# Attention with local and pooled keys, then a two-layer MLP in fp32r pairs: new constants for the order planner, and the first chunk's scores taken from the loaded k rows

## The chip, the cores and the metric

The kernel runs on one core of a Trainium2 chip. The metric is device time in microseconds (us) of one execution; "time before" is the median of three runs. The profile is one further execution of the same program, with its own time.

## The reference

`q`, `k` and `v` have the shape (4 batches, 8 heads, 768 positions, 64). Each row attends to the keys less than 16 positions away and to 24 pooled keys, one for each block of 32 positions. The MLP then runs on the 3072 rows of 512 numbers.

```python
k_sum = k.reshape(B, H, nb, block, D).max(axis=3)      # 24 pooled keys
v_sum = v.reshape(B, H, nb, block, D).mean(axis=3)     # 24 pooled values
scores_l = scale * q @ k.T                             # kept where |i - j| < 16
scores_s = scale * q @ k_sum.T + log(block)
a = softmax(concat([scores_l, scores_s]))
attn = a @ concat([v, v_sum])
h = attn_rows @ w_in                                   # 3072 x 512 @ 512 x 2048
out = max(0.01 * h, h) @ w_out                         # 3072 x 2048 @ 2048 x 512
```

## The kernel before

**Tiling.** The rows are cut into eight chunks `c` of 384 rows, two for each batch. A chunk has four pairs of heads `p` and three tiles of 128 rows, so 12 units `u` of (pair, tile). For a unit, TensorE makes the scores (`scores`, L371): two heads by two half tiles of 64 rows, each 64 by 120, of which 24 columns are pooled keys and 96 are a window of k. VectorE adds the mask and takes the row minimum (`lowest`, L376), ScalarE exponentiates (`expo`, L383), VectorE divides by the sum (L420, L424, L428), TensorE transposes (`turn`, L388), ScalarE copies the result out (`pt`, L439), TensorE multiplies with the values (`values`, L394), and the product is split into a high and a low fp32r part (`xhi` L445 on ScalarE, `xlo` L448 on VectorE).

**Where the 120 keys come from.** `operands` loads q into the tile `k`, and k into a slot of `big` (named `("kn", c, p)`; six slots of 1024 columns, which also take the raw weights and the raw v). `k_max` (L248, VectorE) reduces the k rows to `ksum`. Then two ScalarE copies (`windows`, L315) lay the overlapping windows of k into the tile `k`, and a VectorE copy (`k_s`, L331) puts the pooled keys in front of each window, so that one matmul of 120 columns reads a contiguous run.

**The values.** For the first batch, TensorE averages v (`v_mean_pe`, L284): three loads `("vb", 0, j)` of 512 KB, two matmuls of 512 columns for each, all into one bank, then a ScalarE copy to `vs` (L289). GpSimd spreads the 24 pooled values into the tile `v` of each pair (`load_s`, L327). `values` cannot run for a pair before that copy. The tiles `e` and `pt` have two buffers for pairs of units, so units cannot run far ahead of `values`.

**The MLP.** `mlp` makes `h` (`m1`, L724), gates it, and accumulates the second product (`m2`, L743 to L745), in the parts of `PARTS`. The weights arrive as raw fp32 (`weights`, one load of 512 KB each, `("w", f, 0)` for w_in and `("w", f, 1)` for w_out) and are split into fp32r pairs by three VectorE operations (L680, L687, L693) and two ScalarE operations (L684, L690). From the third batch position on, products of sums are used (`strassen`), which is the larger part of the time.

**What sets the order.** All instructions are put into a list by `Plan`: each has an engine, a cost in ns and a priority. `Plan.order` runs a list schedule once while the program is built: at each step the engine that is free first takes the ready instruction with the lowest priority number. The time that an instruction gets there fixes its place on its engine; on the chip each engine runs its instructions in that order. Loads are all issued from SyncE (SP) in their order. `Plan.LAT` is the latency that the planner adds from one engine's end to a waiting instruction; a load ends 1200 ns after its issue at the earliest, plus its bytes at `rate`, after the loads before it:

```python
if o["size"]:
    dma = max(dma, end + 1200) + o["size"] / o["rate"]
    end = dma
```

The priorities are made of the unit's place (`PLACE`: for each chunk a start and a step), of offsets for each step of chunks 0 and 1 (`OFF`), and of the constants `PL` to `WO`; `LOADS` fixes the order of the first 20 loads outright. In the gaps that the planner expects on TensorE before the first MLP product, `build` puts small matmuls on zeros (L1343, tile `spare`).

Of the kernel before, what the change touches and what calls it, by code (L numbers as in the profile page):

```python
# [23 lines left out]
LK = 120  # L24
# [41 lines left out]
WT = 1.15
W0 = -1.523
WO = 1.029
CUT = 1
WIDE = 12  # L70
OFF = {('rec', 0): (-2.762, -0.036), ('ex', 0): (3.066, -0.083), ('pt', 0): (0.079, -0.747), ('tr', 0): (-2.274, -0.362), ('ttr', 0): (-5.883, 0.424), ('nrm', 0): (0.274, -0.908), ('qk', 0): (-7.35, 0.368), ('xlo', 0): (1.352, 0.149), ('xhi', 0): (-1.785, 0.164), ('av', 0): (-2.699, -0.545), ('pt', 1): (3.776, 0.667), ('xlo', 1): (2.15, -1.485), ('tr', 1): (-0.4, -0.633), ('ttr', 1): (5.204, 0.013), ('qk', 1): (5.855, -0.039), ('av', 1): (-6.304, -0.442), ('ex', 1): (1.869, -0.057), ('nrm', 1): (1.368, -0.059), ('rec', 1): (3.066, -0.235), ('xhi', 1): (-5.461, -0.101)}
LOADS = [('kn', 0, 0), ('q', 0, 1), ('q', 0, 0), ('kn', 0, 1), ('mask',), ('vb', 0, 0), ('kn', 0, 2), ('vb', 0, 2), ('q', 0, 2), ('vb', 0, 1), ('kn', 0, 3), ('w', 0, 0), ('v', 0, 0), ('v', 0, 1), ('q', 0, 3), ('v', 0, 2), ('v', 0, 3), ('w', 1, 0), ('w', 0, 1), ('w', 1, 1)]


class Plan:


    LAT = {"SP": 910.0, "PE": 200.0, "DVE": 130.0, "ACT": 142.0, "POOL": 190.0,
# [5 lines left out]
    def op(self, eng, cost, prio, fn, after=(), use=(), alloc=(), size=0, rate=250.0, port=False):  # L84
# [26 lines left out]
    def order(self):  # L111
# [18 lines left out]
        while any(cand.values()):  # L130
# [14 lines left out]
            if o["size"]:  # L145
                dma = max(dma, end + 1200) + o["size"] / o["rate"]
                end = dma
# [16 lines left out]
def DVE(n, fast=False):  # L164
    return 65 + (0.52 if fast else 1.042) * n
# [6 lines left out]
def build(tc, ctx, a):  # L172
# [126 lines left out]
    def operands(c, p, t, ahead):  # L299
# [36 lines left out]
        ks = [P.op("ACT", ACT(TPC * 96), t - 0.6 + (0 if b else XW), lambda j=j: windows(j), after=[lq, kn_op[kw]], use=[kk, kw]) for j in range(2)]  # L336
# [5 lines left out]
        ks.append(P.op("DVE", DVE(2 * TPC * NS, True), t - 0.5 + (0 if b else KS), k_s, after=[lq, ksum_op[b, p]], use=[kk, ("ksum", b, p)]))  # L342
# [58 lines left out]
    def unit(u):  # L401
# [48 lines left out]
        o = P.op("PE", 480, v + 0.1 + off("qk"), qk, after=k_op[c, p], use=[kk], alloc=[("h", K("s0"), 0), ("h", K("s1"), 0)] if wide else [("s0", K("s0"), 1), ("s1", K("s1"), 1)])  # L450
        z = []
        for h in range(2):
            al = [(x, (x, m), ER) for x in "emz"] if h + u % 2 == 0 else []
            z.append(P.op("DVE", 280, v + 0.2 + off("ttr"), lambda h=h: lowest(u, h, tl[K(f"s{h}")][:, :LK]), after=[o, mask_op] + z[:1] + first_of.get(m, []),
# [3 lines left out]
        rc = P.op("DVE", 120, v + 0.45 + off("rec"), guard, after=e, use=[("z", m)])  # L458
        rc = P.op("DVE", 130, v + 0.5 + off("rec"), rec, after=[rc], use=[("z", m)])
# [937 lines left out]
```

## Time and profile before

| | us |
|---|---|
| median of three runs | 613.66 |
| lowest and highest | 612.68, 614.12 |
| the profiled execution, its own time | 612.7 |
| its span, first to last instruction | 610.9 |

The 1.8 us between the profiled execution's time and its span lie outside the instructions. The profile lists busy time by engine: PE is TensorE's matmuls, PEld its weight loads, DVE VectorE, ACT ScalarE, POOL GpSimd, SP SyncE, whose entries are issues of DMAs. The ends of matmuls are modelled, so their durations overlap: the time that one costs is read from the start of one to the start of the next. An fp32 matmul leaves two entries. Matmuls on zeros count as busy, so PE's busy share alone does not tell how much of its time is work.

### The profile page before, as it was taken

The page shows a single profiled execution, that of the slowest core. Times are in us where ns is not written, and L with a number is a line of the kernel's source. Part 1 is how long each engine was busy: PE and PEld are TensorE (multiplying, and loading weights), DVE is VectorE, ACT ScalarE, POOL GpSimd, SP SyncE. Part 2 cuts the span into 40 slices and gives each one's busy share as a digit, 9 for nine tenths or more (in the row PEclk, how much of TensorE's full clock was granted, in tenths as well). Part 3 has the DMA queues.
Part 4 walks back from the last instruction along what each step waited for, and adds up shares of the span by engine and source line. Part 5 has one row for each costly group of instructions (what it writes and reads, how often), then busy time and mean ns, then how long its engine had stood idle before and what let it go on. Part 6 is the DMA issues. An engine that isn't in the chain of part 4 may idle for free.

```text
span 610.9 us, 12895 instructions
## 1 busy us (share of the span) xinstructions
PE 604.9 (99%) x4676; PEld 540.1 (88%) x4676; DVE 469.7 (77%) x1281; ACT 351.1 (57%) x965; POOL 4.4 (1%) x10
## 2 busy tenths in 40 slices
PE   9999999999999999999999999999999999999997
PEld 6688889889888889999898897989889899999996
DVE  5899999953989995536688875877987783868687
ACT  5899996553776676416466665753717262606060
POOL 0200000000000000000000000000000000000000
PEclk9999999999999999999999999999999999999999
DMA  8898998896878826526497563866757484757552
GB/s 298 245 282 273 288 301 245 269 325 198 288 240 244 252 64 197 167 65 190 120 292 229 175 219 120 280 202 216 257 183 231 143 236 143 237 152 229 156 155 103
DMA packets 82926, 129.99 MB, mean 213 GB/s; under 512 B 7024, under 2 KB 50608, under 8 KB 82864
## 3 DMA queue, kind: packets, MB, share of 16 engines
q1 hardware_dynamic: 82864, 129.18, 68.1%
q8 instruction: 37, 0.61, 0.4%
q14 instruction: 25, 0.20, 0.1%
HBM read 97.72 MB, written 29.36 MB: 208 GB/s over the span
## 4 chain that ended last, share of the span: by engine, by line
PE 91%; DVE 4%; ACT 2%; DMA 1%; issue 0%; SPq 0%; DVEq 0%
PE L L1229 19%; PE h L724 12%; PE X L1090 8%; PE W L1090 8%; PE Z L1090 7%; PE B_a L1040 5%; PE a L744 4%; PE a L745 4%; PE a L743 4%; PE Y L1090 4%; PE B_s L1040 2%; PE B_to L1040 1%; ACT e L383 1%; PE vps L284 1%; DMA big<-in_k_dram 1%; DVE big L687 1%
## 5 line engine op out<-in xcount | busy, mean ns | idle before, releaser
L724 PE MATMUL h<-x,win_hi 128*128 128x384 f32 x320 | 82.7, 339 | 0.0
L383 ACT ACTIVATE e<-e,m 128x120 f32<-128x120 f32 x192 | 73.7, 388 | 3.7 <-DVE m L376 3.5
L1229 PE MATMUL L<-wout_hi,win_hi 128*128 128x512 f32 x168 | 66.5, 396 | 0.0
L1229 PE MATMUL L<-wout_hi,win_lo 128*128 128x512 f32 x168 | 65.7, 391 | 0.0
L1229 PE MATMUL L<-wout_lo,win_hi 128*128 128x512 f32 x168 | 65.6, 391 | 0.0
L724 PEld LDWEIGHTS h<-x,win_hi 128*128 128x128 f32 x320 | 57.6, 188 | 2.3 <-issue 0.2
L724 PE MATMUL h<-x,win_lo 128*128 128x384 f32 x160 | 53.8, 336 | 0.0
L743 PE MATMUL a<-wout_hi,ghi 128*128 128x512 f32 x120 | 48.4, 403 | 0.0
L745 PE MATMUL a<-wout_hi,glo 128*128 128x512 f32 x120 | 47.3, 394 | 0.0
L744 PE MATMUL a<-wout_lo,ghi 128*128 128x512 f32 x120 | 47.1, 392 | 0.1
L1229 PEld LDWEIGHTS L<-wout_hi,win_lo 128*128 128x128 f32 x168 | 31.5, 188 | 6.8
L383 ACT ACTIVATION_READ_ACCUMULATOR e<-e,m 128x1 f32 x192 | 36.7, 191 | 0.0
L1229 PEld LDWEIGHTS L<-wout_lo,win_hi 128*128 128x128 f32 x168 | 31.6, 188 | 5.7
L1229 PEld LDWEIGHTS L<-wout_hi,win_hi 128*128 128x128 f32 x168 | 31.6, 188 | 5.7
L734 DVE TENSOR_TENSOR glo<-gs,ghi 128x384 fp32r<-128x384 f32 x40 | 22.1, 554 | 17.0 <-ACT gs L728 16.3
L731 ACT ACTIVATE ghi<-h 128x384 fp32r<-128x384 f32 x40 | 19.6, 490 | 25.9 <-PE h L724 25.9
L1186 ACT COPY P<-X 128x384 f32<-128x384 f32 x19 | 9.0, 473 | 37.0 <-PE X L1090 36.9
L724 PEld LDWEIGHTS h<-x,win_lo 128*128 128x128 f32 x160 | 30.0, 188 | 0.0
L745 PEld LDWEIGHTS a<-wout_hi,glo 128*128 128x128 f32 x120 | 22.5, 188 | 5.4 <-DVE glo L734 0.4
L315 ACT COPY k<-big 128x288 f32<-128x288 f32 x64 | 24.8, 434 | 4.1 <-DMA big<-in_k_dram 4.0
L744 PEld LDWEIGHTS a<-wout_lo,ghi 128*128 128x128 f32 x120 | 22.6, 188 | 3.9 <-DVE wout_lo L693 0.4
L743 PEld LDWEIGHTS a<-wout_hi,ghi 128*128 128x128 f32 x120 | 22.6, 188 | 3.3
(620 smaller groups left out, 1625.9 us busy)
## 6 DMA issues: line engine op xcount, KB each, us to landing
win_hi<-sums SPq DMA_DIRECT2D x73, 256.0 KB
win_lo<-sums SPq DMA_DIRECT2D x71, 256.0 KB
big<-in_w_dram SPq DMA_DIRECT2D x32, 512.0 KB
sums<-big SPq DMA_DIRECT2D x32, 512.0 KB
v<-in_v_dram SPq DMA_DIRECT2D x32, 288.0 KB
big<-in_k_dram SPq DMA_DIRECT2D x16, 400.0 KB
k<-in_q_dram SPq DMA_DIRECT2D x32, 192.0 KB
wout_hi<-sums SPq DMA_DIRECT2D x21, 256.0 KB
```

Source lines behind the costliest of these rows:

```text
L315: nc.scalar.copy(k, x)
L383: nc.scalar.activation(out=e[:, n], in_=e[:, n], func=AF.Exp, scale=-1.0, bias=m[:, n:n + 1], accum_out=z[:, n:n + 1])
L724: nc.tensor.matmul(h[:, :T], w[:, 512 * f + 128 * k:512 * f + 128 * k + 128], x[:, T * k:T * k + T], start=n == 0, stop=n == 11)
L731: nc.scalar.activation(out=gnew(tag, G("ghi", f)), in_=tl[G("h", f)][:, :T], func=AF.Prelu, alpha=0.01)
L734: nc.vector.tensor_tensor(out=gnew(tag, G("glo", f)), in0=tl[G("gs", f)], in1=tl[G("ghi", f)].bitcast(F32), op=ALU.subtract)
L743: nc.tensor.matmul(o, gh, wout_hi[:, f], start=f == f0, stop=False)
L744: nc.tensor.matmul(o, gh, wout_lo[:, f], start=False, stop=False)
L745: nc.tensor.matmul(o, gl, wout_hi[:, f], start=False, stop=f == f1 - 1)
L1040: nc.tensor.matmul(o[:, x:x + 256], g, w[l], start=fresh and m == 0, stop=m == 5, skip_group_check=True)
L1090: nc.tensor.matmul(o[:, :T], w[:, l, 128 * k:128 * k + 128], x[y][:, T * k:T * k + T], start=start and n == 0, stop=n == 5, skip_group_che ...
L1186: nc.scalar.copy(tmp(K("P1")), ps("X"))
L1229: nc.tensor.matmul(o, g, w[:, f], start=s + m == 0, stop=s == 1 and m == 5)
```

## The change

Three things are done at once.

- The planner's numbers: the end of a load is counted from 1900 ns after its issue instead of 1200, with 60 ns of latency behind it instead of 910, and bytes at 297 per ns instead of 250 (290 for weights). The VectorE costs of `lowest` (280 to 215), of the guard (120 to 90) and of the reciprocal (130 to 90) go down.
- In chunk 0 (`c == 0`), `windows` and `k_s` are left out. `scores` makes each block of 64 by 120 with two matmuls: 96 columns straight from the loaded k rows in `big`, and 24 columns from `ksum`. The scores wait for the two loads and for `k_max`; the slot of `big` and the tile `ksum` are held until they have run. Their planned cost is 640 ns instead of 480.
- `PLACE`, `OFF`, `LOADS` and the constants `CV`, `PG`, `P2` and `PL` to `WO` have new values; `LOADS` begins with other loads. The new numbers and costs hold for the whole program, so that every engine's order can differ.

```diff
-PLACE = {0: (0.0, 1.0), 1: (13.07, 0.61), 2: (24.128751, 0.979249), 3: (33.570341, 0.464868), ...
+PLACE = {0: (-0.56363, 1.023761), 1: (13.941805, 0.493885), 2: (24.006994, 0.724777), 3: (33.542294, 0.443354), ...
...
-VT = -1.915
-KP = -1.757
+VT = -2.297378
+KP = -2.510813
...
-OFF = {('rec', 0): (-2.762, -0.036), ... ('tr', 0): (-2.274, -0.362), ... ('qk', 0): (-7.35, 0.368), ... ('av', 0): (-2.699, -0.545), ...
+OFF = {('rec', 0): (-9.400226, -0.966702), ... ('tr', 0): (2.239967, -0.883064), ... ('qk', 0): (-4.669325, 0.548837), ... ('av', 0): (-0.911237, -0.250157), ...
-LOADS = [('kn', 0, 0), ('q', 0, 1), ('q', 0, 0), ('kn', 0, 1), ('mask',), ('vb', 0, 0), ('kn', 0, 2), ('vb', 0, 2), ('q', 0, 2), ('vb', 0, 1), ('kn', 0, 3), ('w', 0, 0), ('v', 0, 0), ('v', 0, 1), ('q', 0, 3), ('v', 0, 2), ('v', 0, 3), ('w', 1, 0), ('w', 0, 1), ('w', 1, 1)]
+LOADS = [('kn', 0, 2), ('q', 0, 0), ('mask',), ('kn', 0, 0), ('vb', 0, 0), ('kn', 0, 1), ('q', 0, 1), ('vb', 0, 1), ('vb', 0, 2), ('kn', 0, 3), ('q', 0, 2), ('v', 0, 0), ('v', 0, 1), ('w', 0, 0), ('q', 0, 3), ('v', 0, 2), ('v', 0, 3), ('w', 0, 1), ('w', 1, 0), ('w', 1, 1)]
...
-    LAT = {"SP": 910.0, "PE": 200.0, ...
+    LAT = {"SP": 60.0, "PE": 200.0, ...
...
-    def op(self, ..., size=0, rate=250.0, port=False):
+    def op(self, ..., size=0, rate=297.0, port=False):
...
-                dma = max(dma, end + 1200) + o["size"] / o["rate"]
+                dma = max(dma, end + 1900) + o["size"] / o["rate"]
...
-        ks = [P.op("ACT", ACT(TPC * 96), ..., lambda j=j: windows(j), ...) for j in range(2)]
+        ks = [P.op("ACT", ACT(TPC * 96), ..., lambda j=j: windows(j), ...) for j in range(2)] if c else [lq, kn_op[kw], ksum_op[b, p]]
...
-        ks.append(P.op("DVE", DVE(2 * TPC * NS, True), ..., k_s, ...))
+        if c:
+            ks.append(P.op("DVE", DVE(2 * TPC * NS, True), ..., k_s, ...))
...
                 n, w = 128 * i + 64 * j, T + KC * i + LK * j
+                if c == 0:
+                    o = s[h][64 * j:64 * j + 64, col:col + LK]
+                    nc.tensor.matmul(o[:, NS:], k[x, n:n + 64], tl["kn", c, p][x, n:n + LK - NS], start=True, stop=True)
+                    nc.tensor.matmul(o[:, :NS], k[x, n:n + 64], tl["ksum", c, p][x], start=True, stop=True)
+                    continue
                 nc.tensor.matmul(s[h][64 * j:64 * j + 64, col:col + LK], k[x, n:n + 64], k[x, w:w + LK], start=True, stop=True)
...
-        o = P.op("PE", 480, v + 0.1 + off("qk"), qk, after=k_op[c, p], use=[kk], ...)
+        o = P.op("PE", 640, v + 0.1 + off("qk"), qk, after=k_op[c, p], use=[kk, ("kn", c, p), ("ksum", c, p)], ...)
...
-        o = load_op(("w", f, w), ..., size=128 * 4096, rate=290.0)
+        o = load_op(("w", f, w), ..., size=128 * 4096)
```

## Rows read from the trace of the kernel before

**Rows 1.** The page: its head and the busy time of the engines over the whole span.

```profile
span 610.9 us, 12895 instructions
...
PE 604.9 (99%) x4676; PEld 540.1 (88%) x4676; DVE 469.7 (77%) x1281; ACT 351.1 (57%) x965; POOL 4.4 (1%) x10
```

**Rows 2.** Busy time by stretch. Columns: the stretch and its length in us, busy us (and instructions) of PE, PEld, DVE, ACT and POOL, granted TensorE clock, share of the DMA engines' time, GB/s.

```profile
5.00:8.00 3.00, 2.84 (x55) 2.40 (x52) 1.31 (x5) 0.77 (x3) 0.00 (x0) 1.00 1.02 377
8.00:16.00 8.00, 7.85 (x81) 4.09 (x81) 6.04 (x42) 6.67 (x30) 0.00 (x0) 1.00 0.96 330
16.00:21.56 5.56, 5.56 (x46) 2.48 (x46) 4.62 (x20) 3.52 (x13) 0.98 (x2) 1.00 1.03 250
21.56:34.00 12.44, 12.41 (x195) 9.49 (x193) 10.49 (x50) 11.72 (x45) 2.68 (x3) 1.00 0.83 246
34.00:60.00 26.00, 25.92 (x200) 22.19 (x198) 24.92 (x82) 24.80 (x72) 0.00 (x0) 1.00 0.92 281
60.00:100.00 40.00, 40.00 (x283) 35.14 (x282) 39.49 (x94) 35.64 (x82) 0.00 (x0) 1.00 0.93 284
...
233.00:500.00 267.00, 267.00 (x1907) 238.46 (x1906) 191.50 (x483) 142.81 (x383) 0.00 (x0) 1.00 0.63 196
```

**Rows 3.** The same view for the matmuls on zeros alone (L1343). Columns: stretch, length, busy us of PE and of PEld, clock, DMA share, GB/s.

```profile
5.00:21.56 16.56, 5.61 (x87) 4.92 (x84) 1.00 0.99 312
21.56:34.00 12.44, 2.44 (x35) 1.93 (x33) 1.00 0.83 246
```

**Rows 4.** The timeline of PE around the first `values` and the last matmuls on zeros. Columns: start us, length us, engine, line, operation, tiles, shapes, count.

```profile
19.84 1.79 PE L1343 MATMUL spare<-zero 128*128 128x128 bf16 x29
21.56 0.69 PE L394 MATMUL o<-pt,v 120*64 120x64 f32 x16
...
33.21 0.95 PE L1343 MATMUL spare<-zero 128*128 128x128 bf16 x14
33.97 0.63 PE L724 MATMUL h<-x,win_hi 128*128 128x384 f32 x2
```

**Rows 5.** The timeline of the first 24 us: the way from the pooled values' matmuls to the tile `v`. A bracket gives the idle time of the engine before the row and what ended it.

```profile
15.34 1.04 PE L284 MATMUL vps<-big,mask 128*24 128x512 f32 x2
...
18.01 1.90 PE L284 MATMUL vps<-big,mask 128*24 128x512 f32 x4
...
19.94 0.57 ACT L289 COPY vs<-vps 24x512 f32<-24x512 f32 x1 [1.51 <-PE vps L284]
...
20.58 3.66 POOL L327 COPY v<-vs 24x768 f32<-24x768 f32 x4 [19.28 <-ACT vs L289]
```

**Rows 6.** Waits of TensorE's weight loads over the whole span: who waited for whom, us in total, times, longest us.

```profile
PEld B_a L1040 <- DVE y L1051: 0.7, 1, 0.7
```

**Rows 7.** The timeline of the DMA issues on SP.

```profile
4.02 0.56 SPq L278 DMA_DIRECT2D big<-in_v_dram  x1
8.87 0.33 SPq L310 DMA_DIRECT2D k<-in_q_dram  x1
9.24 0.43 SPq L278 DMA_DIRECT2D big<-in_v_dram  x1
...
11.29 0.90 SPq L319 DMA_DIRECT2D v<-in_v_dram  x2
```

**Rows 8.** Bytes of the loads, from the list of DMA issues: count, KB each.

```profile
v<-in_v_dram SPq DMA_DIRECT2D x32, 288.0 KB
big<-in_k_dram SPq DMA_DIRECT2D x16, 400.0 KB
k<-in_q_dram SPq DMA_DIRECT2D x32, 192.0 KB
...
big<-in_v_dram SPq DMA_DIRECT2D x3, 512.0 KB
...
mask<-in_mask_dram SPq DMA_DIRECT2D x1, 202.0 KB
```

**Rows 9.** The first 15 us in the view by stretch, with the columns of Rows 2.

```profile
0.00:5.00 5.00, 4.01 (x48) 4.02 (x49) 1.18 (x3) 2.05 (x3) 0.70 (x6) 1.00 0.65 199
5.00:10.00 5.00, 4.82 (x73) 3.29 (x70) 3.13 (x21) 2.77 (x13) 0.00 (x0) 1.00 1.00 380
10.00:15.00 5.00, 4.87 (x55) 2.90 (x58) 3.64 (x21) 3.67 (x15) 0.00 (x0) 1.00 0.93 311
```

**Rows 10.** The timeline of the start: the first two maxima of k, the first scores and the first mask.

```profile
3.90 0.95 DVE L248 TENSOR_REDUCE ksum<-big 128x24 f32<-128x768 f32 x1 [2.97 <-DMA big<-in_k_dram]
...
5.86 0.64 PE L371 MATMUL s<-k 64*64 64x120 f32 x16
...
6.81 0.95 DVE L248 TENSOR_REDUCE ksum<-big 128x24 f32<-128x768 f32 x1 [1.69 <-DMA big<-in_k_dram]
7.68 0.27 DVE L376 CUSTOM_DVE_ANT_0 e<-s,mask 128x120 f32<-128x120 f32 x1
```

**Rows 11.** ScalarE's groups of instructions between 21.56 and 34 us: the copies that lay out the windows. Columns behind the first bar: busy us, mean ns of one; behind the second: idle time before them.

```profile
L315 ACT COPY k<-big 128x288 f32<-128x288 f32 x4 | 1.6, 437 | 0.0
```

**Rows 12.** VectorE's groups in the same stretch: the copies that lay out the pooled keys.

```profile
L331 DVE COPY k<-ksum 128x144 f32<-128x144 f32 x2 | 0.5, 228 | 0.0
```

**Rows 13.** Two neighbours on PE's timeline: one unit's scores, and what starts behind them.

```profile
23.83 0.44 PE L371 MATMUL s<-k 64*64 64x120 f32 x8
24.20 0.45 PE L394 MATMUL o<-pt,v 120*64 120x64 f32 x8
```

More of the change, by code (lines that the diff above doesn't have):

```diff
@@ L82, in __init__, with op @@
         self.ops, self.rings, self.users, self.slot = [], {}, {}, {}
-    def op(self, eng, cost, prio, fn, after=(), use=(), alloc=(), size=0, rate=250.0, port=False):
+    def op(self, eng, cost, prio, fn, after=(), use=(), alloc=(), size=0, rate=297.0, port=False):
         o = {"eng": eng, "cost": cost, "prio": prio, "fn": fn, "after": list(after), "size": size, "rate": rate, "n": len(self.ops)}
@@ L335, in operands @@
             kn_op[kw] = load_op(kw, t - 1.3 - ahead, load_k, alloc=[("big", kw, 0)], size=128 * (T + 2 * WIN) * 4)
-        ks = [P.op("ACT", ACT(TPC * 96), t - 0.6 + (0 if b else XW), lambda j=j: windows(j), after=[lq, kn_op[kw]], use=[kk, kw]) for j in range(2)]
+        ks = [P.op("ACT", ACT(TPC * 96), t - 0.6 + (0 if b else XW), lambda j=j: windows(j), after=[lq, kn_op[kw]], use=[kk, kw]) for j in range(2)] if c else [lq, kn_op[kw], ksum_op[b, p]]
         lv = load_op(("v", c, p), t - 0.6 - ahead, load_v, alloc=[("v", kv, VR)], size=96 * TPC * 1024)
@@ L341, in operands @@
             ls = P.op("POOL", POOL(2 * TPC * 128), t - 0.3, load_s, after=[lv, vsum_op[b]], use=[kv, ("vsum", b)])
-        ks.append(P.op("DVE", DVE(2 * TPC * NS, True), t - 0.5 + (0 if b else KS), k_s, after=[lq, ksum_op[b, p]], use=[kk, ("ksum", b, p)]))
+        if c:
+            ks.append(P.op("DVE", DVE(2 * TPC * NS, True), t - 0.5 + (0 if b else KS), k_s, after=[lq, ksum_op[b, p]], use=[kk, ("ksum", b, p)]))
         k_op[c, p], v_op[c, p] = ks, [lv, ls]
@@ L448, in xlo @@
             nc.vector.tensor_tensor(out=x_of(xl, c, r, 128), in0=tl[ko][:, :128], in1=x_of(xh, c, r, 128).bitcast(F32), op=ALU.subtract)
-        o = P.op("PE", 480, v + 0.1 + off("qk"), qk, after=k_op[c, p], use=[kk], alloc=[("h", K("s0"), 0), ("h", K("s1"), 0)] if wide else [("s0", K("s0"), 1), ("s1", K("s1"), 1)])
+        o = P.op("PE", 640, v + 0.1 + off("qk"), qk, after=k_op[c, p], use=[kk, ("kn", c, p), ("ksum", c, p)], alloc=[("h", K("s0"), 0), ("h", K("s1"), 0)] if wide else [("s0", K("s0"), 1), ("s1", K("s1"), 1)])
         z = []
@@ L457, in unit @@
         e = [P.op("ACT", ACT(LK, extra=2), v + 0.3 + off("ex"), lambda h=h: expo(u, h), after=[z[h]], use=[("e", m), ("m", m), ("z", m)]) for h in range(2)]
-        rc = P.op("DVE", 120, v + 0.45 + off("rec"), guard, after=e, use=[("z", m)])
-        rc = P.op("DVE", 130, v + 0.5 + off("rec"), rec, after=[rc], use=[("z", m)])
+        rc = P.op("DVE", 90, v + 0.45 + off("rec"), guard, after=e, use=[("z", m)])
+        rc = P.op("DVE", 90, v + 0.5 + off("rec"), rec, after=[rc], use=[("z", m)])
         nm = P.op("DVE", DVE(2 * LK), v + 0.55 + off("nrm"), nrm, after=[rc], use=[("e", m), ("z", m)])
@@ L693, in s5 @@
             nc.vector.tensor_tensor(out=lo, in0=lw(), in1=hi.bitcast(F32), op=ALU.subtract)
-        o = load_op(("w", f, w), t - 0.25 * BIG, load, alloc=[("big", kr, 0)], size=128 * 4096, rate=290.0)
+        o = load_op(("w", f, w), t - 0.25 * BIG, load, alloc=[("big", kr, 0)], size=128 * 4096)
         o0 = o
```

48 lines of the change are left out of this document (24 added, 24 removed).

## The prediction

> **What bounds the kernel now.** I read the page's head first: PE is busy for 604.9 of 610.9 us [rows 1], so that on the face of it nothing is to be had. The view by stretch says where that is true [rows 2]. From 34 us on PE is busy in every us shown, to within 0.08 us of 26, then 40 of 40 and 267 of 267; the last of it is products of the MLP, and an order that hides something else there gains nothing. The same view for the matmuls on zeros alone says where it is not true [rows 3]: they take 5.61 us between 5 and 21.56 and 2.44 us between 21.56 and 34, and PE's timeline has the last of them directly before 33.97 us, where the first MLP product goes on for good [rows 4]. So the end of the program is 33.97 us plus a train of PE work that no longer waits, and the question is how early that train can start: call that point the saturation.
>
> What holds the saturation back is read from the same timeline. The first `values` runs at 21.56 us, behind 1.79 us of zeros from 19.84 on [rows 4]. Before it: two matmuls of the pooled values start at 15.34, the last four entries at 18.01 and end 1.90 us later at 19.91, the copy to `vs` starts at 19.94, GpSimd's spread at 20.58 after 19.28 us of idleness [rows 5]. From the last matmul's end to `values` it is 21.56 - 19.91 = 1.65 us. Until then only four units fit into the two buffers of `e` and `pt`; in the stretch from 16 to 21.56 ScalarE is busy for 3.52 of 5.56 us, afterwards for 11.72 of 12.44 [rows 2]. After the saturation the longest wait of PE's weight loads for another engine is 0.7 us [rows 6].
>
> **The loads.** In SP's list the eighth load goes out at 4.02 us; the ninth, a q, at 8.87, since it waits for a buffer; behind it stands the third load of raw v, at 9.24 [rows 7]. The new list puts all three loads of raw v among the first nine, ahead of the first load that has to wait; that one is the fourth k (for the slot of the first k, now held until unit 2's scores), and behind it wait q, v and the weights. Up to and with the third raw v it is 3 x 400 + 2 x 192 + 202 + 3 x 512 = 3322 KB, 3.40 MB [rows 8]. Before, 199 x 5 + 380 x 5 = 2.90 MB had come by 10 us, then 311 GB/s [rows 9]: the rest takes 1.6 us, 11.6 us in all. The planner now counts 0.55 + 1.9 + 3.40 MB at 297 GB/s = 13.9 us, and as each engine keeps its order, the two last matmuls come between these. With 1.9 us for them and the 1.65 us behind, `values` starts between 15.2 and 17.5 us; I take 16.4. The v rows of the first pair, 400 + 192 + 288 KB further on [rows 8], have come by 10 + (4.30 - 2.90) / 0.311 = 14.5 us and don't set this. Gain at that point: 21.56 - 16.4 = 5.2 us.
>
> **The start gets later.** The new list loads the k rows of pair 2 first and those of pair 0 fourth: 400 + 192 + 202 + 400 = 1194 KB. Before, the fourth load closed 1184 KB and was reduced at 6.81 us. So the first scores, which now wait for the maximum (0.95 us), come near 7.9 instead of 5.86 us. The first mask was at 7.68 only because that second maximum stood ahead of it on VectorE [rows 10]; it comes near 8.5, 0.8 us later. Against this the maximum of pair 2 (0.95 us) is done in idle time at about 3.9 us, and the copies fall away. By 16 us VectorE is then about level with before.
>
> **What is removed.** `windows` for eight copies and `k_s` for four. Of these, four copies of ScalarE, 1.6 us, and two of VectorE, 0.5 us, lie between 21.56 and 34 us, the busy stretch [rows 11, 12]; the others lie where both engines have idle time and cost nothing.
>
> **What is added.** A unit's scores took 24.20 - 23.83 = 0.37 us from start to start [rows 13]. Twice as many matmuls for the same columns: between nothing and another 0.37 us, no row has such a pair. I take half, 0.18, as no row is nearer to either end. For twelve units that is 2.2 us (0 to 4.4). About seven units are scored before 16 us, beside zeros; five, 0.9 us (0 to 1.9), lie behind. The Trainium skill has a rule against this part: TensorEngine Tiling (Array Packing), section Instruction Overhead, gives every matmul about 60 cycles, so that one column costs as much as sixty. By that, 96 + 60 columns in place of 120 would make it 0.48 us a unit, an estimate, and the bound of 0.37 us more would shrink to 0.11. No row here has a matmul that short.
>
> **The sum.** I take what each engine did between 16.0 and 33.97 us before, without zeros and copies, and lay it behind 16.0 us, as what stood idle there waited for `values`. VectorE: 4.62 + 10.49 - 0.5 = 14.6 us, done at 30.6. ScalarE: 3.52 + 11.72 - 1.6 = 13.6, done at 29.6. PE: 5.56 + 12.41 - 1.79 - 2.44 = 13.7, with the scores 14.6 (13.7 to 15.6), done at 30.6 (29.7 to 31.6) [rows 2 to 4]. VectorE and PE end together; I add 0.2 us for the first `values` at 16.4 instead of 16.0, since the work before it is only half held. Saturation 30.8 instead of 33.97 us: 3.2 us less. What comes next is unchanged work on PE; late next are the weights' splits on VectorE, busy there for 24.92 of 26 and 39.49 of 40 us [rows 2], but they are ahead of their use, as the short waits show.
>
> The profiled execution took 612.7 us, 0.96 below the median of the three runs and inside their span. From its own time: 612.7 - 3.2 = 609.5; the same step from the median: 613.66 - 3.2 = **610.5 us**. The new costs also remake the order of everything after the third chunk. There, PE has no idle time worth a tenth of a us in 267 us [rows 2], so that no gain is left; a wait like the one of 0.7 us may come or go, which I put at 0.7 us either way.
>
> **Rivals.**
> (1) The gaps stay. Between 21.56 and 34 us VectorE was busy for 10.49 of 12.44 us, 84%, with work at hand: it waited for ScalarE and PE in turn. If that share holds from 16 us on, 14.6 / 0.84 = 17.4 us, saturation at 33.4 us, 0.6 us less: 613.1. For it: a unit is a chain over three engines and five steps of VectorE. Against it: twelve units and the raw weights are then at hand together, and ScalarE was at 94% in that stretch; it was the one that the others waited for, and it loses 1.6 us.
> (2) Slower: the loads of the weights fall behind the plan. The old plan had 250 GB/s (290 for weights), the new one 297; between 34 and 100 us the trace has 281 and 284 [rows 2]. Over these 66 us that is 26 us at 281 and 40 us at 284 GB/s, 18.7 MB, which the new plan sees done in 62.9 us, 3.1 us too early. Splits that are placed by that stand at the head of VectorE's and ScalarE's queues while their load is under way, and gates and masks queue behind them, and PE behind those. With the start's gain at a third, 1.0 us: 613.66 - 1.0 + 3.1 = 615.8. It decides from the point where the lag passes the saturation's gain, 3.2 us, or, with less gain, sooner. Against it: the DMA engines are at 92 and 93% there and gave 330 and 377 GB/s earlier, so that the rate is partly what was asked for, and the fixed times have become longer by 700 ns and shorter by 850 at the same time.
> (3) The change does not do what it says: matmuls of the pooled values are late for another reason (their order on PE among the scores), `values` stays near 21 us, copies gone and the start later cancel: 613.7.
>
> **Chances.** Forecast 0.63 (saturation between 28.5 and 32.3 us), (1) 0.17, (2) 0.14, (3) 0.06. About 1.2 us, 0.2%, is what a measurement of this kernel can tell from no change. Part of (1) is faster than that, 0.03: faster 0.66, same 0.19, slower 0.15. The range reaches down to 608.2 (613.66 - 4.8 - 0.7: `values` at the early end, 15.2 us, and so the saturation at 29.2, and a wait of 0.7 us gone) and up to 614.2, which holds (1) and (3) and the late ends of the costs, and leaves out (2) and about 0.05 at the lower end.
>
> **What would show it.** Right: zeros end before 32 us; first `values` between 15 and 18 us; no L315 and L331 for chunk 0; PE full from the saturation to 600 us. Wrong: `values` at 20 us or later (the loads' step); zeros until 33 us with `values` at 16 (rival 1); PE gaps between 34 and 110 us behind VectorE or ScalarE that wait for a weight load (rival 2); scores of chunk 0 above 0.74 us a unit (the added matmuls).

## The result, and the profile after

After takes 622.05 us (median of four runs), before beside it 613.64. Three of the four runs of after lie between 620.33 and 623.59 us; the fourth, the profiled one, took 658.75 us at a granted clock of 0.85 throughout and is left out of the ratio. That ratio is 1.0134 [1.0118, 1.0150] (in brackets, here and below, its 95% interval), 8.2 us slower where 3.2 us less was forecast. The rows below are from a further run of the same program, e1, whose clock was 0.999; it took 618.76 us and so, against 612.7 for the profiled run of before, 6.1 us more. These 6.1 us are what rows can explain: e1's profiled run is the fastest of its six (618.76 to 624.01), so that some 2 us of the loss are in no row.

The page's head of e1, answering to [rows 1], and the view by stretch with the columns of [rows 2]:

```profile
span 617.0 us, 12957 instructions
...
PE 605.1 (98%) x4721; PEld 538.5 (87%) x4721; DVE 470.9 (76%) x1277; ACT 346.7 (56%) x957; POOL 4.0 (1%) x10
```

```profile
16.00:21.56 5.56, 5.20 (x84) 3.03 (x82) 3.64 (x23) 4.58 (x21) 2.44 (x3) 1.00 0.95 269
21.56:34.00 12.44, 11.70 (x195) 9.15 (x196) 12.33 (x62) 12.09 (x47) 0.91 (x2) 1.00 0.93 284
34.00:60.00 26.00, 26.00 (x203) 22.60 (x201) 24.49 (x77) 24.43 (x71) 0.00 (x0) 1.00 0.92 283
60.00:100.00 40.00, 37.66 (x271) 33.06 (x270) 39.03 (x90) 33.32 (x78) 0.00 (x0) 1.00 0.92 285
100.00:233.00 133.00, 132.20 (x1084) 116.28 (x1083) 107.25 (x309) 81.72 (x246) 0.00 (x0) 1.00 0.73 230
233.00:500.00 267.00, 266.18 (x1916) 234.31 (x1915) 188.84 (x485) 140.96 (x379) 0.00 (x0) 1.00 0.61 191
```

The loss does not lie where the change's own work lies. Between 21.56 and 34 us VectorE and ScalarE are even fuller than before (12.33 and 12.09 of 12.44 us). But PE, which before was busy for 40.00 of 40 us from 60 us on and 267.00 of 267 later, now lacks 2.34 us between 60 and 100 and 0.8 in each of the two stretches behind.

The start, PE's timeline and then SP's issues, with the columns of [rows 4] and [rows 7]:

```profile
8.02 0.35 PE L374 MATMUL s<-big,k 64*64 64x96 f32 x2 [0.74 <-DMA big<-in_k_dram]
8.91 0.23 PE L375 MATMUL s<-ksum,k 64*64 64x24 f32 x1 [0.55 <-DVE ksum L248]
...
16.78 1.04 PE L284 MATMUL vps<-big,mask 128*24 128x512 f32 x2
17.75 0.43 PE L394 MATMUL t<-ident,e 128*120 128x128 f32 x2
...
19.99 0.69 PE L400 MATMUL o<-pt,v 120*64 120x64 f32 x16 [0.27 <-POOL v L327]
...
33.12 1.07 PE L1349 MATMUL spare<-zero 128*128 128x128 bf16 x16
34.00 0.64 PE L730 MATMUL h<-x,win_hi 128*128 128x384 f32 x2
```

```profile
4.02 1.57 SPq L278 DMA_DIRECT2D big<-in_v_dram  x2
11.20 0.33 SPq L244 DMA_DIRECT2D big<-in_k_dram  x1
```

The raw v loads do go out early, but the first `values` comes at 19.99 us, 1.57 earlier than before, and the last zeros are where they were: the train starts at 34.00 us instead of 33.97. PE's matmuls waited for other engines here:

```profile
PE s_('g', 13, 1)_1302 L400 <- DVE x L545: 1.1, 1, 1.1
...
PE to_('g', 12, 1)_1259 L394 <- ACT ghi L737: 0.8, 1, 0.8
...
PE to_('g', 11, 1)_1152 L394 <- DVE e L528: 0.4, 1, 0.4
PE X L1096 <- ACT P L1192: 0.4, 1, 0.4
```

Before, this list had three entries over the whole span, the longest behind the start 0.5 us. One of the new waits, with VectorE's timeline in front of it: the transposes at 70.10 us wait 0.45 us for the normalisation (L528), which stands behind four pieces of weight splits (L699, twice L693, L686) and the gate's low part (L740):

```profile
66.55 0.69 DVE L699 TENSOR_TENSOR wout_lo<-big,wout_hi 128x512 fp32r<-128x512 f32 x1
67.16 1.29 DVE L693 SCALAR_TENSOR_TENSOR big<-big 128x512 int32<-128x512 int32 x2
...
68.43 0.43 DVE L686 TENSOR_SCALAR big<-big 128x512 int32<-128x512 int32 x1
...
68.86 0.53 DVE L740 TENSOR_TENSOR glo<-gs,ghi 128x384 fp32r<-128x384 f32 x1
69.31 0.65 DVE L528 TENSOR_TENSOR e<-e,z 128x480 f32<-128x480 f32 x1
```

**How the waits are counted below.** For each matmul I take the time from its start to the next start; what exceeds the usual time of the same pair of kinds (its median over the runs; noise up to some 0.06 to 0.17 us is let pass) is a wait. Unlike busy time this also finds short waits, since the modelled ends overlap. It splits the way to PE's last start (606.53 us before, 612.60 in e1) into work, zeros and waits. The table has all runs together (columns of waits: stretches in us); before was run again beside each group and had medians of 613.1 to 613.6. `us` is the median of the timed runs, the waits are of the profiled one alone, whose own time lies up to 2.8 us from that median, so that differences of a us or two between rows tell little. Where the granted clock fell in a run, the slower matmuls count as waits, too (last section). The fixed 2.3 to 2.5 us behind 500 us are the same everywhere and left out.

| | us | ratio to before | zeros | waits 0-36 | 36-110 | 110-233 | 233-500 |
|---|---|---|---|---|---|---|---|
| before | 613.1 to 613.6 | | 11.7 | 0.8 | 1.2 | 1.5 | 1.8 |
| e1 after | 621.40 | 1.0134 | 8.8 | 3.4 | 3.3 | 2.4 | 4.8 |
| e2 scores alone | 622.63 | 1.0144 | 13.4 | 1.2 | 2.7 | 8.5 | 2.0 |
| e3 counts alone | 619.25 | 1.0105 | 11.4 | 4.9 | 4.0 | 2.5 | 3.4 |
| e4 after, old scores | 623.36 | 1.0168 | 12.0 | 4.6 | 3.4 | 2.8 | 3.9 |
| e5 scores, before's order | 613.47 | 1.0001 | 11.9 | 0.3 | 2.9 | 1.4 | 1.9 |
| e6 after, old VectorE counts | 624.84 | 1.0174 | 12.3 | 2.9 | 3.5 | 3.8 | 3.4 |
| e7 VectorE counts alone | 618.29 | 1.0075 | 14.6 | 0.8 | 2.2 | 2.7 | 2.1 |
| e8 one ns | 614.16 | 1.0016 | 13.2 | 0.3 | 1.4 | 1.5 | 2.5 |
| e9 early values | 622.37 | 1.0149 | 10.2 | 10.2 | 1.7 | 1.3 | 2.0 |
| e10 and no zeros | 622.65 | 1.0154 | 7.6 | 11.2 | 3.9 | 1.3 | 2.0 |
| e11 after, PE counts | 616.89 | 1.0059 | 10.6 | 2.2 | 4.6 | 1.4 | 2.4 |
| e12 loads' numbers alone | 621.31 | 1.0133 | 12.7 | 4.1 | 5.0 | 1.6 | 4.1 |
| e13 e11, old loads' numbers | 623.58 | 1.0162 | 12.6 | 1.3 | 1.4 | 8.2 | 2.2 |
| e14 before, PE counts | 620.56 | 1.0111 | 14.0 | 0.9 | 0.7 | 6.8 | 2.0 |
| e15 e11, rate 281 | 618.42 | 1.0077 | 11.7 | 1.5 | 0.7 | 3.9 | 3.2 |
| e16 e15, new tables | 614.69 | 1.0021 | 12.2 | 2.2 | 0.6 | 1.7 | 3.2 |
| e17 e15, other new tables | 613.52 | 1.0004 | 12.3 | 1.0 | 0.6 | 1.4 | 2.2 |
| e18 before, new tables | 615.40 | 1.0026 | 11.0 | 4.1 | 2.9 | 1.4 | 2.0 |

Of e1's 6.1 us more, the zeros give -2.9, the waits up to 36 us +2.6, the matmuls of the scores +0.5 (25.5 to 26.0); the waits behind 36 us give 2.1 + 0.9 + 2.9 = +5.9 (from unrounded values). The start is level; the train has become longer.

### The profile page after: what moved, and what is told of

Read it like the earlier page. It is cut to its first block, busy times and chain, and to the rows that moved or that the text cites. A ratio compares the mean times of both kernels' runs of the same rounds, so it can differ in the third digit from the quotient of the medians.

```text
span 657.0 us, 12957 instructions
## 1 busy us (share of the span) xinstructions
PE 649.6 (99%) x4721; PEld 566.9 (86%) x4721; DVE 475.6 (72%) x1277; ACT 350.1 (53%) x957; POOL 4.1 (1%) x10
## 4 chain that ended last, share of the span: by engine, by line
PE 95%; DVE 2%; DMA 2%; issue 0%; ACT 0%; SPq 0%; ACTq 0%
PE L L1235 19%; PE h L730 14%; PE W L1096 7%; PE X L1096 7%; PE Z L1096 7%; PE B_a L1046 5%; PE a L749 5%; PE a L751 5%; PE a L750 5%; PE Y L1096 4%; PE B_s L1046 2%; PE B_to L1046 2%; PE vps L284 1%; DMA big<-in_k_dram 1%; DMA big<-in_vb_dram 1%
## 5 line engine op out<-in xcount | busy, mean ns | idle before, releaser
L730 PE MATMUL h<-x,win_hi 128*128 128x384 f32 x320 | 88.1, 358 | 0.0
L1235 PE MATMUL L<-wout_hi,win_hi 128*128 128x512 f32 x168 | 71.4, 425 | 0.0
L1235 PE MATMUL L<-wout_hi,win_lo 128*128 128x512 f32 x168 | 70.1, 417 | 0.0
L1235 PE MATMUL L<-wout_lo,win_hi 128*128 128x512 f32 x168 | 70.0, 416 | 0.0
L730 PE MATMUL h<-x,win_lo 128*128 128x384 f32 x160 | 56.7, 355 | 0.0
L749 PE MATMUL a<-wout_hi,ghi 128*128 128x512 f32 x120 | 51.1, 426 | 0.0
L751 PE MATMUL a<-wout_hi,glo 128*128 128x512 f32 x120 | 50.1, 417 | 0.0
L750 PE MATMUL a<-wout_lo,ghi 128*128 128x512 f32 x120 | 50.0, 417 | 0.0
L740 DVE TENSOR_TENSOR glo<-gs,ghi 128x384 fp32r<-128x384 f32 x40 | 22.1, 553 | 24.5 <-ACT gs L734 23.2
L1144 ACT ACTIVATE win_hi<-U 128x384 fp32r<-128x384 f32 x28 | 14.6, 523 | 45.1 <-DVE U L1132 45.0
L1257 DVE TENSOR_TENSOR rows<-L,rows 128x512 f32<-128x512 f32 x18 | 12.4, 691 | 20.7 <-PE L L1235 20.7
```

Of the source, the lines that this page charges most:

```text
L730: nc.tensor.matmul(h[:, :T], w[:, 512 * f + 128 * k:512 * f + 128 * k + 128], x[:, T * k:T * k + T], start=n == 0, stop=n == 11)
L740: nc.vector.tensor_tensor(out=gnew(tag, G("glo", f)), in0=tl[G("gs", f)], in1=tl[G("ghi", f)].bitcast(F32), op=ALU.subtract)
L749: nc.tensor.matmul(o, gh, wout_hi[:, f], start=f == f0, stop=False)
L750: nc.tensor.matmul(o, gh, wout_lo[:, f], start=False, stop=False)
L751: nc.tensor.matmul(o, gl, wout_hi[:, f], start=False, stop=f == f1 - 1)
L1144: nc.scalar.activation(out=hi, in_=ps("X") if direct else tl[kt], func=AF.Prelu, alpha=0.01)
```

## The experiments

The edits are given in short, partly in words; `...` stands for what is left out.

**Which part?** My first theory was the clock of the first profile; the rivals were the order of the lists and the new scores. e1 repeats after; e2 and e3 put one part each into before; e4 puts the old scores back into after.

```diff
# e2: before, with the change's scores, their cost and without chunk 0's copies; e4: after, with the old ones
-        ks = [P.op("ACT", ..., windows(j), ...) for j in range(2)]
+        ks = [...] if c else [lq, kn_op[kw], ksum_op[b, p]]
# e3: before, with the change's planner numbers
-    LAT SP 910, 1200 ns, 250 (weights 290) per ns; lowest 280, guard 120, reciprocal 130
+    LAT SP 60, 1900 ns, 297 per ns; 215, 90, 90
```

> The changed kernel as it is, for a profile at full clock: the one at hand was granted 0.851 throughout. Clock theory: TensorE loses time because the granted clock is below 1.0 in some stretch (its other executions show a mean of 0.998 to 0.999, the kernel before 1.000); then most of the 7 to 8 us stand in rows at a clock below 1.00, and PE waits no more than before after the saturation. Order theory: clock 1.00 in every stretch that matters, and the 7 to 8 us are PE gaps behind VectorE, ScalarE or loads. Rival 2 of the prediction (loads of the weights behind the plan): the gaps lie between 34 and 110 us. Time 620 to 622 in all of them.

> The kernel before with only the chunk 0 scores taken from the loaded k rows (planned cost 640, no copies), old counts and old tables. If the two matmuls in place of one cost PE time on the path: 614 to 617. If what is removed weighs more: 612 to 613.5. If they alone bring the clock down: 620.

> The kernel before with only the planner's new counts (loads, latency of SP, three VectorE costs), old scores and old tables. Loads theory (rival 2): slower by 2 us or more, with PE gaps between 34 and 110 us. Otherwise within 2 us of before, either side, as the tables were not made for these counts.

> The changed kernel with the old scores and copies put back, counts and tables new. If the scores cause the loss: 611 to 615. If the tables or counts cause it: 619 to 624, about as the changed kernel.

Measured: 621.40 [1.0113, 1.0154], 622.63 [1.0129, 1.0159], 619.25 [1.0091, 1.0118] and 623.36 [1.0155, 1.0182]. The clock falls out: e1 has 1.00 in every stretch up to 500 us. But the parts don't add up either: each alone costs 6 to 9 us, and without the scores after is no faster. e2 lies above all three of its ranges; e3 fits the theory of the loads (4.0 us of waits between 36 and 110 us). What e2, e3 and e4 have in common with after is that every list was planned anew.

**The instructions or their order?** e5 has the change's scores in before's order: the list is planned as in before, with the twelve copies as empty places, and only loads into slots that the new scores still read are put behind those scores; each engine's own order stays that of before. e8 changes no part at all, but one planned cost by 1 ns; 67 of PE's 491 pieces and 175 of VectorE's 1088 then stand elsewhere. e6 and e7 try a first idea of what a bad order is made of: that the plan lost its slack on VectorE.

```diff
# e5: before, scores as in after; windows and k_s of chunk 0 planned, not emitted
+    todo = P.order(), and a load behind the scores that still read its slot
# e6: after
-    lowest 215, guard 90, reciprocal 90
+    lowest 280, guard 120, reciprocal 130
# e7: before, the other way round; e8: before
-    lowest 280
+    lowest 279
```

> The kernel before with the change's scores in chunk 0 and without the eight windows and four k_s copies there, but in the order of before: the list is planned with before's numbers as if the copies were still there, and only loads that need a slot of big which chunk 0's scores still read are put later (three loads of SP by a few places). If the order is the cause (theory A): what is left is the direct price of the new scores and copies, 612.5 to 614.5 us, PE waits behind 36 us as before (1.2 us between 36 and 110 us). If the new scores and the held slots are the cause by themselves (theory B): 618 to 623 us, as with the new scores in a new order (622.6).

> The kernel after with VectorE's planned costs as before (lowest 280, guard 120, reciprocal 130); loads' numbers, tables and scores of after. Theory A1 (the plan lost its slack on VectorE, and the chip falls behind it between 34 and 110 us): PE's waits between 36 and 110 us go from 3.3 to 1.2 to 1.8 us, and the time to 617 to 619.5 us. Theory A2 (any other order than before's costs about as much, whatever the numbers): 618.5 to 624 us, and the waits sit anywhere.

> The kernel before with VectorE's new planned costs alone (215, 90, 90). Theory A1: VectorE falls behind its plan between 34 and 110 us, PE's waits there grow from 1.2 to 2.5 to 4 us, and the time is 616 to 619 us. If it is the loads' numbers that cost the 5.9 us of the counts alone: 613 to 614.5 us. Theory A2: 618 to 623 us, with waits anywhere.

> The kernel before with one planned cost 1 ns lower (lowest 279 instead of 280): no count becomes truer and no slack is lost, but 67 of PE's 491 and 175 of VectorE's 1088 planned pieces take another place in their engine's list. Theory A1: 613 to 615 us. Theory A2: 617 to 623 us.

Measured: e5 613.47 [0.9991, 1.0011]: the new scores cost and gain nothing in before's order, and the loss lies in the order (theory A). Its profiled run, at 614.63 the slowest of the ten, has 2.9 us of waits between 36 and 110 us where 1.2 were expected. e8 614.16 [1.0003, 1.0029]: a small shuffle by itself costs about 1 us, so that "any other order costs 5 us" falls as well. e7 618.29 [1.0056, 1.0095] has the time that the slack theory asked for, but not its reason: VectorE does not fall behind e7's list (it is 1.2 us ahead of it at 72 us), the waits between 36 and 110 us are 2.2 us where 2.5 to 4 were expected, 2.9 us more are zeros, and the list itself plans 5.2 us of idleness for PE between 36 and 233 us, before's 1.3. e6 is the clear miss: 624.84 [1.0145, 1.0203] where the theory asked for 617 to 619.5. Slack on VectorE is neither shown as the cause nor does it mend the order.

**The forecast's own step.** e9 takes e5 and brings the third raw v load, the last pooled matmuls and the copy forward, without the zeros in front; e10 leaves out the later zeros too.

```diff
# e9: e5, and
+    the load of the third raw v before the q of pair 2
+    the last four pooled matmuls around the second unit's transposes
+    the copy to vs before the first ScalarE piece planned at 17.6 us or later
-    zeros between the sixth unit's scores and the first values
# e10: e9, and
-    zeros up to the first steady MLP product
```

> The new scores in the order of before (613.47 us), with four things moved and nothing else: the third load of raw v goes ahead of the q that waits for a buffer; the last four matmuls of the pooled values go ahead of the second and third units' transposes; the copy to vs goes ahead of the exponentials that stood before it; and the zeros between the sixth unit's scores and the first values (2.9 us) are left out, those behind it stay. This is the loads' step of the prediction by itself. Prediction's step (start of the train follows the first values): values near 18 us instead of 21.6, the first MLP product's steady train 1.5 to 3 us earlier, 611 to 612 us. Rival (VectorE is the second bound up to 110 us; it stood idle for only 8.15 us in all between 5 and 110 us, and what the start gains is given back in waits behind it): values near 18 us, and the time 613 to 614.5 us. Rival (gaps stay): values near 18 us, zeros or waits fill the same stretch, last of them at 33 us or later.

> As the run with the early values, and the zeros between the first values and the first steady MLP product (2.4 us by the trace of before) are left out as well, so that nothing but a wait can hold TensorE there. If those zeros held TensorE up: 1 to 2.4 us below the run with them. If they only fill waits: equal within 0.5 us, with PE waits of the same length in their place; should the granted clock fall behind such a wait, longer.

Measured: 622.37 [1.0132, 1.0166] and 622.65 [1.0139, 1.0169], worse than every expectation. PE's timeline of e9:

```profile
14.28 1.04 PE L286 MATMUL vps<-big,mask 128*24 128x512 f32 x2 [1.01 <-DMA big<-in_v_dram]
...
15.62 2.75 PE L286 MATMUL vps<-big,mask 128*24 128x512 f32 x6
...
22.95 0.69 PE L403 MATMUL o<-pt,v 120*64 120x64 f32 x16 [0.93 <-POOL v L330]
...
28.35 0.70 PE L403 MATMUL o<-pt,v 120*64 120x64 f32 x8 [4.23 <-DVE x L457]
```

and ScalarE's:

```profile
21.46 0.56 ACT L291 COPY vs<-vps 24x512 f32<-24x512 f32 x1
```

The third raw v lands at 14.2 us, although it is issued before 5.4. The pooled matmuls end near 18.3, and the copy to `vs` waits in ScalarE's list until 21.46 behind exponentials that are now late themselves. Then VectorE works through the split of the first weights before `xlo` (28.02 us), and PE stands for 4.23 us. So e9 did not give early `values`, and what they would be worth was not measured; it shows what a load and five pieces moved by hand do to the other lists. e10 is level with it: the zeros only filled waits.

**Which counts?** The planner's time of each piece can be set beside the trace. VectorE runs ahead of before's list by 1.3 us at 34 us and 2.0 at 100; in e1 it is behind its list by 1.3 us at 34, 2.7 at 72 and 3.8 at 100. The list of before leaves PE 1.3 us of idleness behind 36 us, that of after none, so my idea was that nothing absorbs the lag. (The lag by itself does not tell the waits: in e11, below, it is 7.4 us at 100 us, and PE waits less than in e1.) And the counts are not all true: the attention pieces of PE are planned at 91.0 us in after, their starts in e1 give 74.3 (scores 26.0, `values` 27.3, transposes 21.0). VectorE and loads were made shorter, PE left long, so that the list gives VectorE more time beside PE than there is. e11 sets PE's counts to what the trace of after shows (behind chunk 0 units are planned in pairs, later in quads); e12 puts the loads' numbers alone into before; e13 takes them back in e11, e15 changes the rate alone; e14 gives before PE's counts of e11 alone.

```diff
# e11: after; e14: before, with 480 -> 370 for the unit
-    scores of a unit 640; pairs 758, 600, 600; quads 1280, 510, 1340
+    scores of a unit 430; pairs 570, 410, 560; quads 1000, 410, 1085
# e12: before; e13: e11, the other way round
-    LAT SP 910, 1200 ns, 250 (weights 290) per ns
+    LAT SP 60, 1900 ns, 297 per ns
# e15: e11
-    rate=297.0
+    rate=281.0
```

> The kernel after with TensorE's planned costs of the attention pieces set to what the trace of after shows (unit's scores 430 for 640; pair 570, 410, 560 for 758, 600, 600; quad 1000, 410, 1085 for 1280, 510, 1340). In after VectorE's and the loads' counts were made shorter and these were left long, so that the plan gives VectorE more time beside TensorE than there is. If that imbalance is the cause of PE's waits: waits behind 36 us go from 12.7 us to 8 or less, and the time to 614 to 618 us. If any order made anew without slack costs as much: 619 to 625 us.

> The kernel before with the loads' numbers of the change alone (60 ns, 1900 ns, 297 per ns for all). With VectorE's costs alone it took 618.3 us, with both 619.3. If the loads' numbers carry part of the loss (rival 2 of the prediction: splits placed by loads that land later): 616 to 620 us, with ScalarE or VectorE waiting for weight loads for 2 us and more between 34 and 115 us. If they carry none: 613 to 615 us.

> The kernel after with TensorE's true counts (616.89 us) and the loads' numbers of before (910, 1200, 250 and 290 for weights). In the run with TensorE's counts alone 4.6 us of PE's waits lay between 36 and 110 us, the longest (1.5 us at 89.5) at the end of a chain from a weight load through ScalarE and VectorE to the second product. If the loads' numbers cause those (rival 2 of the prediction): waits there of 1.2 to 2 us, ScalarE waits for weight loads for less than 2.5 us between 85 and 112 us, and the time is 613 to 615.5 us. If they do not: 616 us or more with the same chain.

> The kernel before with TensorE's true counts for the attention pieces (370 for 480, the pairs and quads as in the other run) and nothing else: VectorE's masks stay at 280 and the loads long. If true counts are good by themselves: 611 to 613.5 us. If it is the balance between the engines that counts, and VectorE's and the loads' counts are now too long beside TensorE's: the plan leaves TensorE idle behind 110 us, and the time is 614 to 619 us.

> The kernel after with TensorE's true counts and the loads' rate at 281 bytes per ns, which the trace of before shows between 34 and 60 us, instead of 297; the fixed times stay as in after. If the rate is what is wrong with the loads' numbers: waits between 36 and 110 us of 1.5 to 3 us and 613.5 to 616 us. If it is the fixed times or the order at large: 616 to 620 us.

Measured: e11 616.89 [1.0043, 1.0075], more than half of the loss gone; behind 110 us the waits go from 7.2 to 3.8 us. The time is as expected, the waits are not: all that lie behind 36 us, the fixed ones among them, went from 12.7 to some 10.7 us, where 8 or less was expected. Between 36 and 110 us e11 waits for weight loads; its chain of waits there:

```profile
80.05 7.06 DMA big<-in_w_dram
...
87.13 0.69 ACT big L690
87.82 0.55 ACT win_hi L696
...
89.69 1.20 DVE big L693 x2
...
91.75 0.47 DVE glo L740
...
92.27 0.79 PE a L751
```

A weight load takes 7.06 us, ScalarE's and VectorE's splits wait for it, the gate's low part stands behind them, and PE behind that. e12 (621.31 [1.0084, 1.0182], above its range) has 5.0 us of waits in this stretch; with the old loads' numbers (e13, 1.4 us) or the rate of 281 (e15, 0.7 us) they are gone. After itself is another case: in e1 ScalarE and VectorE waited for weight loads for 1.9 us between 36 and 110 us, less than in before (2.4 us; e11 8.2, e12 4.5), and the chain of waits of e1 from 60 to 82 us holds work of the two engines alone, mostly splits, and no load. The view by stretch, of e15 in two stretches and of e13 in the second:

```profile
60.00:100.00 40.00, 40.00 (x283) 35.11 (x282) 38.70 (x90) 32.83 (x77) 0.00 (x0) 1.00 0.90 279
100.00:233.00 133.00, 131.19 (x1078) 115.19 (x1077) 108.27 (x311) 83.50 (x248) 0.00 (x0) 1.00 0.74 234
```

```profile
100.00:233.00 133.00, 128.01 (x1001) 112.52 (x1003) 104.85 (x286) 76.52 (x224) 0.00 (x0) 0.97 0.74 232
```

But the times miss: 623.58 [1.0133, 1.0190] and 618.42 [1.0051, 1.0103], and e14 is 620.56 [1.0083, 1.0138], above both of its ranges. In all three, waits have come between 213 and 220 us; in e13 the longest, 2.65 us, stands before the scores of quad 12, which wait for the copies of the windows and of the pooled keys (L315, L331). Their lists hold that hole themselves: PE's planned idleness between 110 and 233 us is 11.0, 7.6 and 4.4 us in e13, e14 and e15 (0.7 in before), the measured waits 8.2, 6.8 and 3.9; likewise 5.4 and 8.5 in e2. The tables in them were not chosen with these counts.

**Tables that fit the counts.** e16 and e17 keep e15's counts and choose `PLACE`, `OFF`, `LOADS` and the constants anew: each candidate's list was played through, every engine in its order, with the durations of the traces, and the shortest kept. e18 does so for before.

```diff
# e16, e17: e15; e18: before
-    PLACE, OFF, LOADS and the constants CV to WO
+    the same names with numbers of the search
```

> The kernel with the change's scores, TensorE's true counts and loads at 281 bytes per ns (618.42 us with the change's tables), with tables (PLACE, OFF, LOADS and the constants) chosen anew: by a search that played each list through with the durations of the traces, several sets of them, and took the one with the least end. If it is the fit of tables, counts and chip to each other that decides: the waits at 213 to 218 us go and the time is 612 to 615 us, perhaps below before. If a new order costs 4 us and more whatever is done: 617 us or more.

> The same search from another start, with other tables in the end, played through to the same length within 0.1 us. It tells how far two orders that look equal differ on the chip: within 1 us of the other if the durations tell the time, 3 us or more apart if they do not.

> The kernel before with its own counts and scores, and only its tables chosen anew by the same search; played through, it ends 0.9 us earlier than with before's tables. If the durations tell the time: 611.5 to 613.5 us. If before's tables fit the chip in ways that the durations do not hold: 615 us or more.

Measured: 614.69 [1.0011, 1.0031], 613.52 [0.9994, 1.0014] and 615.40 [1.0009, 1.0043]. PE of e17 by stretch:

```profile
60.00:100.00 40.00, 40.00 (x259) 35.78 (x259) 39.58 (x92) 34.34 (x80) 0.00 (x0) 1.00 0.93 291
100.00:233.00 133.00, 133.00 (x1088) 117.04 (x1088) 108.89 (x310) 83.57 (x247) 0.00 (x0) 1.00 0.72 228
233.00:500.00 267.00, 267.00 (x1934) 237.51 (x1933) 191.54 (x495) 144.08 (x387) 0.00 (x0) 1.00 0.64 197
```

The changed kernel with PE's counts and the loads' rate from the traces and with tables chosen anew is level with before in e17, 1.3 us slower in e16, and the train of e17 has no hole left. So a new order need not cost 8 us. Whether the counts or the search did it is not separated: after's own counts with tables from the same search were not run, and e18, which keeps before's counts, comes to 1.6 us above before, about where e16 is. Two lists that look equal differ by 1.2 us on the chip, and e18 had looked 0.9 us better than before: below 2 to 3 us the durations do not tell which list is better. No version beat before.

## Why the prediction was wrong

**The train.** The failed step is the first one: "33.97 us plus a train of PE work that no longer waits", and with it "0.7 us either way" for the new order behind the third chunk. That PE did not wait was a property of before's order, not of the work. The train grew by 6.0 us, 5.9 of them waits. The same instructions in before's order (e5) lose nothing, and e17's other order has PE busy in every us from 34 to 500. VectorE shows why an order could lose so much: it was busy for 24.92 of 26 and 39.49 of 40 us before [rows 2], which I read as "ahead of their use", when it was a second bound without slack.

**The first `values`.** Forecast 16.4, measured 19.99. The loads' step (third raw v at 11.6 us, by the plan at most 13.9, then two matmuls) failed twice. In e9 and e10, where PE waited for the third raw v, it landed at 14.2 and 13.8; in e1 it was there by 15.45 at the latest. The bytes came about as the sum had them, 3.46 MB of loads up to 12 us in e9, but PE waited for the third raw v until 3.99 MB had come, bytes of the q and k issued behind it among them. And PE was no longer idle: from 8.91 us on it worked through six units' scores, all six pooled matmuls and two units' transposes, up to 17.75. The pooled matmuls had become part of a full queue.

**The start.** It was forecast to leave VectorE "about level with before" at 16 us, with the first scores near 7.9 us and the first mask near 8.5. The first scores are at 8.02, but that is luck: the k rows landed only then, the maximum ran from 7.91 to 8.86, the second half of the scores came at 8.91 and the first mask at 9.41 instead of 7.68 before. VectorE's timeline, and its masks up to 16 us, of e1 and below it of before:

```profile
7.91 0.95 DVE L248 TENSOR_REDUCE ksum<-big 128x24 f32<-128x768 f32 x1 [2.80 <-DMA big<-in_k_dram]
9.41 0.28 DVE L382 CUSTOM_DVE_ANT_0 e<-s,mask 128x120 f32<-128x120 f32 x1 [0.56 <-PE s L375]
```

```profile
L382 DVE CUSTOM_DVE_ANT_0 e<-s,mask 128x120 f32<-128x120 f32 x8 | 2.0, 274 | 0.6 <-PE s L375 0.6
```

```profile
L376 DVE CUSTOM_DVE_ANT_0 e<-s,mask 128x120 f32<-128x120 f32 x14 | 3.5, 275 | 0.0
```

A unit has two masks: four units were masked instead of seven, and what was missing had to be done behind 16 us.

**The saturation.** Forecast 30.8, measured 34.00. VectorE worked 3.64 + 12.33 = 16.0 us between 16 and 34 where the sum had 14.6 from 16.0 on. Six masks of the late start are 1.2 us of that, at 0.20 us each from start to start. A misread row adds to it: of the copies between 21.56 and 34 us [rows 11, 12] only two of the four on ScalarE and one of the two on VectorE are chunk 0's, so that 0.8 and 0.2 us fell away, not 1.6 and 0.5; the others are chunk 1's and still run. VectorE stood idle for 1.9 us between 16 and 21.56 (0.9 before) and gained that back behind (0.1 us idle for 1.95). The sum took 16.0 us as the point from which all engines would be full; VectorE was full from 21.56 on. The lower end of the range does not come out of the sum either: with `values` at 15.2 us its 14.6 us of VectorE end at 29.8 us or later, not at 29.2.

**Right was** the sign of the scores' price. A unit took 24.29 - 23.86 = 0.43 us in e5 against 0.37 [rows 13], so 0.06 more, not 0.18:

```profile
23.86 0.41 PE L375 MATMUL s<-big,k 64*64 64x96 f32 x8
...
24.29 0.45 PE L401 MATMUL o<-pt,v 120*64 120x64 f32 x8
```

The Trainium skill (TensorEngine Tiling (Array Packing), Instruction Overhead) would have given 0.11, which was nearer than my middle. In e5 the removed copies, this price and the later start come to nothing together.

**The rivals.** (2), weight loads behind a plan at 297 GB/s and PE gaps between 34 and 110 us, was priced at 3.1 us and given 0.14. Its gaps are there, 2.1 us more than before in e1 and 3.8 in e12, and they go when the plan's rate does (e15). Its chain from a late load to PE is shown in e11 and e12 alone: in e1 the engines waited no longer for weight loads than before. The larger part of the loss, 3.8 us of waits behind 110 us, stood in no rival; e11 shows that it shrinks when PE's planned costs do. (1) came near the saturation (33.4 us), but not by its reason: VectorE was busy for 16.0 of 18.0 us, 89% and not 84%, with more work than the sum had. (3) was nearly right about `values` and named the order of PE's list as a reason; neither held the end.

**Open.** That the order costs the 8 us is shown; what in after's order does it is not. The 2.9 us more of waits between 233 and 500 us were not followed to their causes. Why e6 and e13, each with part of the old counts, are worse than after was not taken apart beyond the holes in their lists; and what early `values` alone would be worth, since e9 did not produce them.

## What to carry to other kernels

When a list schedule is planned with counted durations, correcting some of them can cost time, as the tables were chosen with the old ones: VectorE's alone cost 5 us, the loads' alone 8, TensorE's alone 7, and with tables chosen anew 0 to 1.3 us were left. "The bound engine never waits" belongs to an order and not to a kernel; before costing a change that makes the order anew, look for the engine that is nearly full beside it, and ask what keeps the bound one fed. And put a change into the old order first (e5): it told in one experiment that the instructions were innocent.

## What had not been expected of the hardware

Where PE had waited a good deal, the granted clock fell, and it took its time to come back, so that a wait cost more than its length. In e9 PE was busy for 2.50 of the 4 us before 24 us, in e2 for 2.27 of the 4.5 before 220.5; behind that the clock stood at 0.50 and 0.52; 0.50 is 1.2 GHz, the lower of its two levels. The stretches 20 to 34 us of e9, and 216 to 227.5 of e2, with the columns of [rows 2]:

```profile
20.00:24.00 4.00, 2.50 (x61) 1.96 (x54) 2.90 (x17) 3.63 (x17) 1.92 (x3) 0.99 0.45 130
24.00:28.00 4.00, 0.13 (x2) 0.00 (x0) 3.25 (x9) 1.46 (x5) 0.62 (x1) 0.50 0.04 13
28.00:34.00 6.00, 5.65 (x70) 4.16 (x70) 3.17 (x19) 3.33 (x14) 0.82 (x1) 0.50 0.66 221
```

```profile
216.00:220.50 4.50, 2.27 (x39) 1.51 (x37) 3.86 (x19) 4.40 (x19) 0.00 (x0) 1.00 0.53 165
220.50:227.50 7.00, 5.05 (x44) 4.75 (x45) 6.89 (x24) 2.85 (x8) 0.00 (x0) 0.52 0.54 166
```

In e9 the clock was 0.70 from 34 to 40 us and 1.00 again from 40 on. What the lower level costs can be read in e11, where PE waited for 1.35 us before 91.21 and the clock was 0.57 from 92 to 96 us. The same products start every 0.23 us before that wait and every 0.42 or 0.43 us behind it:

```profile
84.15 0.39 PE L749 MATMUL a<-wout_hi,ghi 128*128 128x512 f32 x1
84.38 0.39 PE L750 MATMUL a<-wout_lo,ghi 128*128 128x512 f32 x1
...
91.21 0.50 PE L749 MATMUL a<-wout_hi,ghi 128*128 128x512 f32 x1 [1.35 <-ACT ghi L737]
...
92.86 0.63 PE L749 MATMUL a<-wout_hi,ghi 128*128 128x512 f32 x1
93.28 0.63 PE L750 MATMUL a<-wout_lo,ghi 128*128 128x512 f32 x1
```

e12 (0.61 from 82 to 86 us), e13 (0.77 from 220 to 230) and e14 (0.57 from 219 to 223) have such stretches, too, so that part of their waits in the table is this. In e1, whose longest wait behind the start is 1.1 us, the clock stayed at 1.00.
